# Moving the second token block's divisions among the first block's output products, and reordering copies, additions and loads in the first feed-forward units

## The chip, the core and the metric

The kernel runs on one core of one Trainium2 chip. Its five engines are named as in the profile: PE (TensorE, matrix products; PEld is its weight load), DVE (VectorE), ACT (ScalarE), POOL (GpSimd) and SP (SyncE, which here issues most of the DMAs). The metric is the device time of one execution in microseconds (us). Each engine runs its own list of instructions strictly in order and waits at semaphores for the others; a DMA queue, too, is served by an engine that waits in order before it issues.

## The reference

Two branches read the same `x` (2048 tokens, D = 576) and are mixed by a gate per token:

```python
g = _sigmoid((x * gate_w).sum(-1, keepdims=True))
a = _A_ref(x, A_wqkv, A_w_phi, A_wo)
b = _B_ref(x, B_W_gate, B_W_up, B_W_down)
return g * a + (1 - g) * b
```

`_A_ref` is linear attention with 32 heads of 18. Queries and keys go through a small matrix per head, `w_phi`, and become features `phi = concat(softmax(p), softmax(-p))`. Then `kv = phi_k^T v`, `z = sum phi_k`, `o = (phi_q kv) / (phi_q z + 1e-6)`, and the result is `o @ wo`. `_B_ref` is a gated unit of width F = 4608: `relu(x W_gate) * (x W_up)`, times `W_down`. Everything is float32.

## The kernel before, in words

**Split products.** A float32 operand is cut into a high part (a copy in the reduced format `fp32r`, made by ACT) and a low part (operand minus high part, made by DVE), and one product becomes three matmuls: high by high, high by low, low by high. So before any operand can be multiplied, an ACT copy and a DVE subtraction have to be done.

**Attention.** Tokens are handled in tiles of 128 and blocks of 512 (`TB`). There are four blocks, taken in the order `BLOCKS = (3, 0, 1, 2)`; below "block b" is the b-th of that order, so b = 0 is the first one finished. For each block:
- `sums(b, ...)` (L553 to L574) multiplies the turned query features with the key-value matrix in six groups, ACT copies numerators and denominators out of PSUM, and SP moves the denominators into the tile `dn` by DMA.
- `gather(b, ...)` (L576 to L587) moves leftover numerator rows to their place, by SP's DMAs.
- `invert(b)` (L596 to L601) makes the reciprocals on DVE and sends them to `kt` by a DMA of SP; `split_inverse(b)` (L603 to L616) splits them on POOL into the tile `rd` (for b = 0 the low part is made by DVE).
- `divide(b, k)` for k = 4, 3, 2, 1, 0 is `quotient` (one matmul with `spread`, L634, that lays the reciprocals out over 128 rows, and one DVE product `R`, L636) and `operand_rows` (ACT's high part `oh`, L643, and DVE's low part, L644: `ol` for k < 4, the lower half of `oh` for k = 4). The matmul's PSUM bank is `kv_bank(0)`, except that block 1's last division, k = 0, takes `kv_bank(1)`; later blocks alternate between the two.
- Block 0's output products are accumulated in five banks `PW[0]` to `PW[4]` at once: `first_out(k, mm)` (L652 to L657) multiplies by the weights of row group k for each m of `mm`. `PW[0]` and `PW[1]` are the halves of one PSUM tile `two`; `PW[2]` and `PW[3]` are `kv_bank(1)` and `kv_bank(2)`. `rows_out(b, m, ps)` (L791 to L800) copies a finished bank out on ACT (`o`, L796 and L798; for m = 4 DVE adds two halves, L799) and stores it in the DRAM tile `att`. The other blocks use `project_out(b, m)`, all k in one go, L175.

Meanwhile the last query tiles are finished: `final = query_steps(FIRST - 1)` is a generator with the steps projection; maxima and minima; subtraction and exponentials; and finally sum (`sm`, L204), reciprocals (L357, L358) and scaling (`e`, L209). `hg = half_gates(1)` (L301 to L314) makes square roots of the gate for the second half of the tokens: an ACT square root (L308), which needs its table loaded, and some small DVE operations.

**Feed-forward.** The hidden dimension is cut into 36 chunks, and tokens into two halves of 1024, which gives 72 units. A unit multiplies with seven products instead of eight (a Strassen-like scheme of block sums, order `SEQ = (1, 5, 6, 2, 7, 3, 4)`), so `step(u, j)` has j = 0 to 6. Product 1 goes to a new bank `cx`, 5 to `ca`, 2 to `cy`; 6, 7 and 4 are added to `cx`, 3 to `ca`. Between them the running sums are taken out: `g1` is a copy of `cx` after j = 0 (ACT, L1299, traced at j = 1), `u2` one of `ca` (j = 2), `g2` one of `cx` (j = 3); DVE adds `cy` to `g1` (L1418, j = 4), `cx` to `u2` (L1420, j = 5), `ca` to `g2` (L1423, j = 6), and gates them (L1295). PE may not write the next product into a bank before it is read. In the same step the next unit's weights are made: `blocks` (high part `wb`, L874, and low parts L877 and L880), `sums_of_blocks` (four DVE operations on `wr`, L895 to L898) and `block_sums` (`ws`, same lines). They are kept in DRAM (`wbd`, `wsd`) for the second half. The weight tiles `wb` and `ws` have two buffers each, so unit 2's take those of unit 0. From unit 2 on, the down product of a pair of units is added (`ac`, L1179) to the accumulators, which are first loaded from `att` by `load_acc` (L1141) and `load_rest` (L1146), into the buffers that held the output projection's weights.

The seven token operands of the first half are made during the last projections: `operand_ahead(i)` for i = 0 to 2, `high_in_place(0, i)` (ACT, L856 and L857) and `low_of_place(i)` (DVE, L861 and L841) for i = 3 to 6; `in_place(6)` is both.

**What sets the order.** A planner with estimated durations orders the instructions of each engine, starting from the order of the program text. `in_order(tc, nc, engines...)` pins the listed engines to the order of the text: in the attention part around the change these are PE, SP and POOL, so that DVE and ACT are left to the planner; from `project_out(2, 1)` on, all five are pinned. `after(tc, nc, engine, *firsts)` only says that what is traced inside stands behind the given instructions on that engine, and `last_of(nc, engine)` is the last one traced.

Of the kernel before, what the change touches and what calls it, by code (L numbers as in the profile page):

```python
# [83 lines left out]
def gated_mix_kernel(  # L84
# [603 lines left out]
    with in_order(tc, nc, nc.tensor, nc.sync, nc.gpsimd):  # L688
        F_ = lambda: whole(late[0])
        run(key_steps, t - 1, (T_(t - 3, 2),), T_(t - 3, 1), F_, K_(t - 3), T_(t - 3, 0))  # L690
        run(query_steps, t - 1, (), F_, T_(t - 2, 2))
        run(key_steps, t, (T_(t - 2, 1),), V_(t - 1, 0), F_, K_(t - 2), T_(t - 2, 0), V_(t - 1, 1))
        run(query_steps, t, (V_(t, 0),), V_(t, 1), F_, K_(t - 1), T_(t - 1, 2), K_(t))
        kv_out()
        A2.close()
        PP.append(RS.enter_context(tc.tile_pool(name="ph1", bufs=1, **R_)))
        kb = RS.enter_context(tc.tile_pool(name="kb", bufs=1, **R_))
        rb = RS.enter_context(tc.tile_pool(name="rb", bufs=2, **R_))
        table = kb.tile([QK, P], F32, name="table")[:, :QG + 4]
        nc.sync.dma_start(table, mask_d)  # L700
        mask, hm, eps = table[:, :QG], table[:, QG:QG + 3], table[:, QG + 3:]
        kvm = kb.tile([QK, NQ * QM + 64], F32, name="kvm")[:, :NQ * QM].rearrange("p (g c) -> p g c", g=NQ)
        nc.gpsimd.memset(kvm, 0.0)
        fetch(BLOCKS[1])
        turn2 = lambda u, b: turn(u, b, kv_bank(2)[:QK].rearrange("p (g t) -> p g t", g=4))

        def middle():
            next(late[0])
            next(late[0])
            turn(t - 1, 1)  # L710
            for q in (2, 1, 0):
                kv_turn(q)

        last = query_steps(FIRST - 2, middle, nc.vector)
        next(last)
        for q in (2, 1, 0):
            kv_blocks(q)
        hg = half_gates(1)
        next(hg)
        turn(t - 1, 0)  # L720
        whole(late[0])
        turn2(t, 2)
        turn(t, 1)
        turn2(t, 0)
        next(last)
        next(last)
        two = pp.tile([P, 2, TB], F32, name="po", tag="pp")
        sums(0, (4,), (kv_bank(0),))
        sums(0, (5,), (kv_bank(1),))
        sums(0, (3, 2), (two[:, 0], two[:, 1]))  # L730
        gate_rows()
        sums(0, (1,), (kv_bank(2),))
        sums(0, (0,), (pv1.tile([P, TB], F32, name="po", tag="pv1"),))
        whole(last)
        turned = lambda ps: ps[:QK].rearrange("p (g t) -> p g t", g=4)
        turn_all(FIRST - 2, [(0, turned(kv_bank(0))), (1, turned(kv_bank(1))), (2, turned(kv_bank(2)))])
        final = query_steps(FIRST - 1, eng=nc.vector)
        next(final)
        gather(0, 4)
        invert(0)  # L740
        gather(0, 3, 2, 1, 0)
        inverse = split_inverse(0)
        next(inverse)
        fetch(BLOCKS[2], nc.gpsimd)
        store_turned(FIRST - 2, nc.gpsimd)
        two = pp.tile([P, 2, TB], F32, name="po", tag="pp")
        sums(1, (4,), (kv_bank(0),))
        sums(1, (5,), (kv_bank(1),))
        halves = last_of(nc, nc.scalar), last_of(nc, nc.vector)
        sums(1, (3, 2), (two[:, 0], two[:, 1]))  # L750
        next(final)
        next(final)
        exps = last_of(nc, nc.scalar)
        whole(inverse)
        divide(0, 4)
        sums(1, (1,), (kv_bank(2),))
        sums(1, (0,), (pv1.tile([P, TB], F32, name="po", tag="pv1"),))
        divide(0, 3)
        two = pp.tile([P, 2, TB], F32, name="pw", tag="pp")
        PW = [two[:, 0], two[:, 1], kv_bank(1), kv_bank(2), pv1.tile([P, TB], F32, name="pw", tag="pv1")]  # L760
        first_out(4, range(5))
        divide(0, 2)
        gather(1, 4)
        with after(tc, nc, nc.vector, last_of(nc, nc.vector)):
            invert(1)
        gather(1, 3, 2, 1, 0)
        with after(tc, nc, nc.vector, halves[1]):
            whole(final)
        first_out(3, range(5))
        two = pp.tile([P, 2, TB], F32, name="po", tag="pp")  # L770
        operands(BLOCKS[3])
        turn_all(FIRST - 1, [(2, turned(kv_bank(0))), (0, turned(two[:, 0])), (1, turned(two[:, 1]))])
        divide(0, 1)
        with after(tc, nc, nc.scalar, exps, halves[0]), after(tc, nc, nc.vector, halves[1]):
            whole(hg)
        A.close()
    L_ = dict(reuse_waits="tile")
    xo = ctx.enter_context(tc.tile_pool(name="xo", bufs=3, **L_))
# [173 lines left out]
    with in_order(tc, nc, nc.tensor, nc.sync, nc.gpsimd):  # L952
# [5 lines left out]
        sums(2, (4, 5), halves)  # L958
        divide(0, 0)
        first_out(1, range(3))  # L960
        sums(2, (3, 2), halves)
        first_out(1, range(3, 5))
        sums(2, (1, 0), halves)
        gather(2, 4)
        for m in range(5):
            first_out(0, (m,))
            rows_out(0, m, PW[m])
            if m in (0, 1, 3):
                divide(1, (4, 3, None, 2)[m])
        divide(1, 1)  # L970
        divide(1, 0)
        with after(tc, nc, nc.vector, last_of(nc, nc.vector)):
            invert(2)
        gather(2, 3, 2, 1, 0)
# [24 lines left out]
    with in_order(tc, nc, nc.tensor, nc.vector, nc.scalar, nc.gpsimd, nc.sync):  # L999
# [36 lines left out]
        sums_of_blocks(1)  # L1036
        high_in_place(0, 4)
        project_out(3, 2)
        block_sums(1, high_w)
        low_of_place(4)  # L1040
        high_in_place(0, 5)
        project_out(3, 3)
        low_parts(block_sums, 1)
        low_of_place(5)
        in_place(6)
        project_out(3, 4)
    AP.close()
    BS.close()
# [278 lines left out]
    def step(u, j):  # L1327
# [60 lines left out]
        if make:  # L1388
            if j == 0:
                blocks(v, high_w)  # L1390
                if v + 1 < NC:
                    load_w(v + 1)
            elif j == 1:
                blocks(v, low_w)
                blocks(v, low_w_rows)
            elif j == 2:
                if v < NC - 2:
                    nc.sync.dma_start(wbd[v], WB.pop(v).bitcast(F32))
                sums_of_blocks(v)
            elif j == 4:  # L1400
                block_sums(v, low_w)
                block_sums(v, low_w_rows)
            elif j == 5:
                if v < NC - 2:
                    nc.sync.dma_start(wsd[v], WS.pop(v).bitcast(F32))
        elif j == 0 and NC < u < 2 * NC - 1:
            load_operands(v)
# [10 lines left out]
            tt(out=T["g1"], in0=cy, in1=T["g1"], op=ADD)  # L1418
        elif j == 5:
            tt(out=T["u2"], in0=cx, in1=T["u2"], op=ADD)  # L1420
        elif j == 6:
            a = T["g2"]
            tt(out=a, in0=ca, in1=a, op=ADD)  # L1423
# [24 lines left out]

        swap_in(u, j)
        if u == 0:  # L1450
            if 3 <= j < 5:
                plain_down(0, (high, low)[j - 3])
            elif j == 5:
# [2 lines left out]
        if u == 1 and j < 2:  # L1456
            (nc.sync.dma_start(wbd[u], WB.pop(u).bitcast(F32)) if j == 0 else
             nc.sync.dma_start(wsd[u], WS.pop(u).bitcast(F32)))
        if u == 1 and j == 6:
            for i in range(8):  # L1460
                load_acc(0, i // 2 % 2, i // 4, i % 2)
            load_rest(0)
        if u in (NC + 1, 2 * NC - 1) and j < 4:
            if j % 2 == 0:
                rest_copy(j // 2)
# [172 lines left out]
```

## Time and profile before

| | us |
|---|---|
| median of 3 runs | 1583.54 (1583.13 to 1584.26) |
| the profiled execution | 1582.98 |
| its span, first to last instruction | 1581.2 |
| PE busy in the span | 1567.2 |
| DVE busy | 1189.2 |
| ACT busy | 558.6 |
| granted TensorE clock | 1.00 |

Times inside the execution are counted from the start of the span. In a row of the timeline the first number is the start, the second the duration, `out<-in` the tiles written and read, `xN` how many instructions are merged into the row, and the bracket the idle time of the engine before it and what ended that. The attention part around the change runs from about 250 to 290 us, the projections of blocks 1 to 3 up to 338 us, and the feed-forward units from there to the end; each unit has 49 matmuls of `SEQ`, and from unit 2 on the down products come between them.

### The profile page before, as it was taken

Reading aid. Unit: us, or ns where it says so; the run is one execution under the profiler, and the core shown is the slowest. Engines: PE = TensorE matmul, PEld = TensorE weight load, DVE = VectorE, ACT = ScalarE, POOL = GpSimd, SP = SyncE. Lnnn points to the kernel's source line nnn. Section 1 sums busy time; section 2 is a strip of 40 time slices with the busy share of each in tenths; the row PEclk is TensorE's granted clock in tenths of the full one; section 3 lists DMA queues with packets and bytes.
Section 4 is the critical chain, followed back from the end, with each engine's and each line's share of the span. In section 5 each row is a group of like instructions: output and inputs, shape, how many; then the busy total and the mean of one; then the engine's idle time right before and its main releaser. Section 6 shows DMA issues by size and latency. Waiting matters only on the chain.

```text
span 1581.2 us, 20182 instructions
## 1 busy us (share of the span) xinstructions
PE 1567.2 (99%) x7823; PEld 1311.4 (83%) x7823; DVE 1189.2 (75%) x1865; ACT 558.6 (35%) x918; POOL 175.1 (11%) x243
## 2 busy tenths in 40 slices
PE   9999999999999999999999999999999999999998
PEld 9999995677888888888888888888888888888887
DVE  4997775597787877887777777777767777777777
ACT  4344335563333333333333334232232322232321
POOL 0126521110000000000000002111111111111110
PEclk9999999999999999999999999999999999999999
DMA  5365315597755575556545516543443443543432
GB/s 172 108 214 185 146 50 158 168 350 253 256 201 212 212 278 204 201 212 224 196 172 206 220 44 236 191 183 132 153 183 132 162 160 131 178 159 132 185 136 75
DMA packets 64539, 283.38 MB, mean 179 GB/s; under 512 B 6802, under 2 KB 17298, under 8 KB 55740
## 3 DMA queue, kind: packets, MB, share of 16 engines
q1 hardware_dynamic: 61228, 270.34, 47.1%
q0 software_dynamic: 2352, 10.11, 1.9%
q10 hardware_dynamic: 864, 1.65, 0.3%
q8 instruction: 61, 1.00, 0.3%
q14 instruction: 34, 0.28, 0.1%
HBM read 172.07 MB, written 108.60 MB: 178 GB/s over the span
## 4 chain that ended last, share of the span: by engine, by line
PE 95%; DVE 3%; ACT 1%; DMA 0%; issue 0%; POOL 0%; SPq 0%; ACTq 0%; POOLq 0%
PE cx L1133 28%; PE ca L1133 14%; PE pd L1173 12%; PE pd L1196 10%; PE cy L1133 7%; PE kv L175 4%; PE pk L175 3%; PE pq L175 3%; PE pm L1173 2%; PE pm L1196 2%; PE kv L421 1%; PE po L562 1%; PE pv L237 1%; PE ptr L379 1%; PE pw L175 1%; PE psf L259 1%
## 5 line engine op out<-in xcount | busy, mean ns | idle before, releaser
L1238 ACT ACTIVATE hh<-g 128x512 fp32r<-128x512 f32 x195 | 120.0, 624 | 457.3 <-DVE g L1295 287.9
L1211 DVE TENSOR_TENSOR ac<-pd,ac 128x512 f32<-128x512 f32 x238 | 163.9, 689 | 144.4 <-PE pd L1196 144.2
L1133 PE MATMUL cx<-xo,ws 128*128 128x512 f32 x1008 | 252.0, 389 | 1.6 <-ACT g L1299 1.6
L1133 PE MATMUL ca<-xo,ws 128*128 128x512 f32 x1008 | 251.9, 389 | 0.0
L1133 PE MATMUL cx<-xo,wb 128*128 128x512 f32 x1008 | 249.0, 389 | 1.5 <-DVE u L1420 1.5
L1133 PEld LDWEIGHTS cx<-xo,ws 128*128 128x128 f32 x1008 | 189.2, 188 | 41.2 <-ACT g L1299 2.1
L1133 PEld LDWEIGHTS cx<-xo,wb 128*128 128x128 f32 x1008 | 188.2, 188 | 42.4 <-DVE u L1420 1.9
L1133 PEld LDWEIGHTS ca<-xo,ws 128*128 128x128 f32 x1008 | 189.2, 188 | 39.3
L1173 PE MATMUL pd<-hh,wd 128*128 128x512 f32 x576 | 200.7, 389 | 0.0
L1196 PE MATMUL pd<-hh,wd 128*128 128x512 f32 x476 | 185.2, 389 | 0.0
L1179 DVE TENSOR_TENSOR ac<-pd,ac 128x512 f32<-128x512 f32 x144 | 99.0, 688 | 105.6 <-PE pd L1173 102.8
L1243 DVE TENSOR_TENSOR hl<-g,hh 128x512 fp32r<-128x512 f32 x195 | 135.4, 694 | 1.9 <-ACT hh L1238 0.2
L1299 ACT ACTIVATE g<-cx 128x512 f32<-128x512 f32 x144 | 85.0, 590 | 129.2 <-PE cx L1133 129.1
L1173 PEld LDWEIGHTS pd<-hh,wd 128*128 128x128 f32 x576 | 108.1, 188 | 22.5
L1133 PE MATMUL cy<-xo,wb 128*128 128x512 f32 x504 | 125.9, 389 | 0.0
L1096 ACT ACTIVATE wd<-wdr 128x384 fp32r<-128x384 f32 (+1 forms) x106 | 62.3, 606 | 143.2 <-DMA wdr<-wd 143.2
L1173 PE MATMUL pd<-hl,wd 128*128 128x512 f32 x288 | 112.0, 389 | 0.0
L1133 PEld LDWEIGHTS cy<-xo,wb 128*128 128x128 f32 x504 | 94.6, 188 | 19.6
L1196 PEld LDWEIGHTS pd<-hh,wd 128*128 128x128 f32 x476 | 89.4, 188 | 18.5
L1196 PE MATMUL pd<-hl,wd 128*128 128x512 f32 x238 | 92.6, 389 | 0.0
L841 POOL TENSOR_TENSOR xo<-xr,xo 32x512 fp32r<-32x512 f32 x5 | 8.3, 1670 | 614.7 <-PE ca L1133 608.5
L874 ACT ACTIVATE ws<-wr 128x1536 fp32r<-128x1536 f32 x36 | 53.7, 1491 | 48.2 <-DVE wr L898 46.0
(256 smaller groups left out, 2572.1 us busy)
## 6 DMA issues: line engine op xcount, KB each, us to landing
wsd<-ws SPq DMA_DIRECT2D x34, 1280.0 KB
ws<-wsd SPq DMA_DIRECT2D x34, 1280.0 KB
wbd<-wb SPq DMA_DIRECT2D x34, 960.0 KB
wb<-wbd SPq DMA_DIRECT2D x34, 960.0 KB
wr<-wgu SPq DMA_DIRECT2D x36, 768.0 KB
wdr<-wd SPq DMA_DIRECT2D x36, 576.0 KB
eT<-et SPq DMA_DIRECT2D x10, 594.0 KB
xt<-xb SPq DMA_DIRECT2D x7, 768.0 KB
```

The costliest lines, as they stand in the source:

```text
L175: nc.tensor.matmul(ps, w, m, start=i == 0, stop=i == len(pairs) - 1)
L237: nc.tensor.matmul(pv[i][c], m, w_[:, k, cs], start=k == 0 and n == 0, stop=k == 4 and n == 1)
L874: nc.scalar.activation(o[:, :, 0:3], a, AF.Copy)
L1096: nc.scalar.activation(o[:, 0], a, AF.Copy)
L1133: nc.tensor.matmul(ps, w, v, start=first and m == 0, stop=m == len(pairs) - 1, skip_group_check=True)
L1173: nc.tensor.matmul(ps, w, v, start=k == 0 and (i < 2 or first), stop=k == len(mms) - 1 and (i < 2 or last), skip_group_check=True)
L1179: tt(out=a, in0=ps, in1=a, op=ADD)
L1196: mm = lambda ps, w, v, a, z: nc.tensor.matmul(ps, w, v, start=a, stop=z, skip_group_check=True)
L1211: tt(out=a, in0=ps, in1=a, op=ADD)
L1238: nc.scalar.activation(h, src, AF.Copy)
L1243: tt(out=l, in0=src, in1=h.bitcast(F32), op=SUB)
L1299: nc.scalar.activation(a, ps, AF.Copy)
```

## The change

It has two parts. In the attention part, block 1's divisions k = 4 and k = 3 move ahead, each in front of a `sums(2, ...)`, and the remaining three go behind m = 0, 2 and 4 of block 0's last products; the copy of `PW[0]` is traced behind the product into `PW[1]`. The rest of `final` is held on DVE behind the first division of block 0 (`split`) instead of behind an earlier operation; the rest of `hg` is traced before block 0's division k = 1 and held behind `split` and behind the ACT copy of the division k = 2 (`rows`).

In the feed-forward part, operand 5's ACT copies move in front of operand 4's DVE work and of block sums 1; `in_place(6)` moves from the last projections into unit 0 (j = 1); in unit 1 the low parts of block sums 2, and their store, move from j = 4 and 5 to behind the addition into `u2` at j = 5; and the ten loads of the accumulators move from the end of unit 1 (j = 6) to the start of unit 0 (j = 0).

```diff
@@ -746,13 +746,12 @@
         sums(1, (4,), (kv_bank(0),))
         sums(1, (5,), (kv_bank(1),))
-        halves = last_of(nc, nc.scalar), last_of(nc, nc.vector)
         sums(1, (3, 2), (two[:, 0], two[:, 1]))
         next(final)
         next(final)
-        exps = last_of(nc, nc.scalar)
         whole(inverse)
         divide(0, 4)
+        split = last_of(nc, nc.vector)
         sums(1, (1,), (kv_bank(2),))
...
         first_out(4, range(5))
         divide(0, 2)
+        rows = last_of(nc, nc.scalar)
         gather(1, 4)
...
         gather(1, 3, 2, 1, 0)
-        with after(tc, nc, nc.vector, halves[1]):
+        with after(tc, nc, nc.vector, split):
             whole(final)
         first_out(3, range(5))
...
+        with after(tc, nc, nc.scalar, rows), after(tc, nc, nc.vector, split):
+            whole(hg)
         divide(0, 1)
-        with after(tc, nc, nc.scalar, exps, halves[0]), after(tc, nc, nc.vector, halves[1]):
-            whole(hg)
         A.close()
...
         sums(2, (4, 5), halves)
         divide(0, 0)
         first_out(1, range(3))
+        divide(1, 4)
         sums(2, (3, 2), halves)
         first_out(1, range(3, 5))
+        divide(1, 3)
         sums(2, (1, 0), halves)
         gather(2, 4)
         for m in range(5):
             first_out(0, (m,))
-            rows_out(0, m, PW[m])
-            if m in (0, 1, 3):
-                divide(1, (4, 3, None, 2)[m])
-        divide(1, 1)
-        divide(1, 0)
+            if m > 0:
+                for i in (0, 1) if m == 1 else (m,):
+                    rows_out(0, i, PW[i])
+            if m in (0, 2, 4):
+                divide(1, 2 - m // 2)
...
         high_in_place(0, 4)
         project_out(3, 2)
+        high_in_place(0, 5)
+        low_of_place(4)
+        project_out(3, 3)
         block_sums(1, high_w)
-        low_of_place(4)
-        high_in_place(0, 5)
-        project_out(3, 3)
         low_parts(block_sums, 1)
         low_of_place(5)
-        in_place(6)
         project_out(3, 4)
...
             elif j == 4:
-                block_sums(v, low_w)
-                block_sums(v, low_w_rows)
+                if u > 1:
+                    block_sums(v, low_w)
+                    block_sums(v, low_w_rows)
             elif j == 5:
-                if v < NC - 2:
+                if 2 < v < NC - 2:
                     nc.sync.dma_start(wsd[v], WS.pop(v).bitcast(F32))
...
         elif j == 5:
             tt(out=T["u2"], in0=cx, in1=T["u2"], op=ADD)
+            if u == 1:
+                block_sums(v, low_w)
+                block_sums(v, low_w_rows)
+                nc.sync.dma_start(wsd[v], WS.pop(v).bitcast(F32))
...
         if u == 0:
+            if j == 0:
+                for i in range(8):
+                    load_acc(0, i // 2 % 2, i // 4, i % 2)
+                load_rest(0)
+            elif j == 1:
+                in_place(6)
             if 3 <= j < 5:
                 plain_down(0, (high, low)[j - 3])
...
-        if u == 1 and j == 6:
-            for i in range(8):
-                load_acc(0, i // 2 % 2, i // 4, i % 2)
-            load_rest(0)
```

## The prediction, made before the changed kernel was run

> **What bounds the kernel now.** I read the page first: the engines' busy shares.
>
> ```profile
> PE 1567.2 (99%) x7823; PEld 1311.4 (83%) x7823; DVE 1189.2 (75%) x1865; ACT 558.6 (35%) x918; POOL 175.1 (11%) x243
> ```
>
> TensorE (PE) is the bound, and the change neither adds nor removes a matmul. It can only fill or open holes in PE's row, so next come PE's two longest waits after its start, and the busy time by stretches.
>
> ```profile
> PE cx L1133 <- ACT g L1299: 1.6, 1, 1.6
> PE cx L1133 <- DVE u L1420: 1.5, 1, 1.5
> ```
> ```profile
> 338.00:365.00 27.00, 23.86 (x105) 19.07 (x104) 21.94 (x31) 13.95 (x21) 1.09 (x2) 1.00 0.76 308
> 365.00:1560.00 1195.00, 1195.00 (x5272) 988.45 (x5271) 908.66 (x1423) 386.31 (x637) 81.95 (x158) 1.00 0.50 182
> ```
>
> The second column of the lower fence is PE's busy time: from 365 us on it has no hole, so a hole removed before that stays won. Both waits lie where the diff edits, and so do those of some 0.5 that the timeline shows with their full size. Fourteen matmuls of 512 columns in 3.34 us, the last lasting 0.39, make a pitch of (3.34 - 0.39)/13 = 0.227 us. Whatever lies between two starts beyond 0.227 per matmul is lost.
>
> ```profile
> 277.28 0.40 PE L634 MATMUL kv<-rd,spread 128*128 128x512 f32 x1
> 278.22 0.50 PE L657 MATMUL pw<-oh,wo 128*128 128x512 f32 x1 [0.55 <-ACT o L796]
> ...
> 281.16 0.40 PE L657 MATMUL pw<-ol,wo 128*128 128x512 f32 x1
> 281.88 0.74 PE L634 MATMUL kv<-rd,spread 128*128 128x512 f32 x2 [0.32 <-DVE R L636]
> ...
> 284.09 0.40 PE L175 MATMUL kv<-oh,wo 128*128 128x512 f32 x1
> 285.02 0.50 PE L175 MATMUL kv<-oh,wo 128*128 128x512 f32 x1 [0.53 <-ACT oh L643]
> 285.74 0.50 PE L175 MATMUL kv<-ol,wo 128*128 128x512 f32 x1 [0.23 <-DVE ol L644]
> ...
> 287.09 1.93 PE L562 MATMUL po<-ph,kvm 108*64 108x512 f32 x6
> ...
> 349.76 3.34 PE L1133 MATMUL cx<-xo,wb 128*128 128x512 f32 x14
> ```
>
> Lost here: 0.94 - 0.23 = 0.71 before 278.22, 0.49 before 281.88, 0.70 and 0.49 before 285.02 and 285.74. That is **2.4 us** in the loop of the first block's last output products.
>
> **Part 1: the second block's divisions** (k = 4 and 3 go ahead of two `sums(2, ...)`, the other three to m = 0, 2, 4). One division is one matmul, three operations of 0.6 to 0.7 us on DVE and ACT, and no DMA; SP and POOL are not touched. Two spread matmuls (0.23 each) move 3 to 6 us ahead in PE's order, which costs nothing in total; their operand `rd` comes from POOL:
>
> ```profile
> 269.04 1.29 POOL L612 TENSOR_TENSOR rd<-kt,rd 32x512 fp32r<-32x512 f32 x1
> 271.39 1.08 PE L562 MATMUL po<-ph,kvm 108*64 108x512 f32 x4
> ```
>
> It is done at 270.3, and PE would come to the spread where `sums(2, (3, 2))` now starts, at 271.4; 1 us is left. What each hole turns into:
> - 0.71: PE waited for the copy `o` of bank PW[0], which shares a tile with PW[1]. Now both copies are traced behind both products. The wait goes.
> - 0.49: the spreads of k = 2 and k = 1 use one bank back to back; now two products (1.4 us) lie between, against 0.4 of matmul and 0.68 of DVE. Gone.
> - 1.19: the projection of block 1 reached k = 1 and 0 before their quotients were split. Now only k = 0 comes last: 0.4 matmul, 0.7 `R`, 0.6 `oh`, 0.7 `ol` = 2.4 us, against eleven matmuls of the projection ahead of it, 2.5 us. Just covered.
> What is late next is ACT: five copies `o` and three `oh` at 0.60 (the row of `g` in part 3) are 4.8 us, while PE has 14 products and 3 spreads, 3.9 us, and eleven matmuls more, 2.5, before it needs the last. If they come in a bad order, PE waits for PW[2] or PW[3] by up to 1 us. So this part gives 1.5 to 2.6 (2.4 and the refill after each hole); I take **2.2**, near the upper end, because each cover is there by the rows.
>
> **Part 2: the tail of `final` and `hg`, held behind the first division.**
>
> ```profile
> 255.36 0.50 PE L634 MATMUL kv<-rd,spread 128*128 128x512 f32 x1
> 256.32 1.20 PE L657 MATMUL pw<-oh,wo 128*128 128x512 f32 x4 [0.45 <-DVE oh L644]
> ...
> 258.72 0.39 PE L657 MATMUL pw<-oh,wo 128*128 128x512 f32 x1
> 259.19 0.50 PE L657 MATMUL pw<-ol,wo 128*128 128x512 f32 x1
> ```
> ```profile
> 254.21 1.33 DVE L204 TENSOR_REDUCE sm<-e 128x64 f32<-128x1152 f32 x1
> 255.58 0.69 DVE L644 TENSOR_TENSOR oh<-R,oh 64x512 fp32r<-64x512 f32 x1
> ```
> ```profile
> 256.10 1.28 ACT L308 ACT_TABLE_LOAD   x1
> 257.39 0.21 ACT L308 ACTIVATE gates<-gates 128x8 f32<-128x8 f32 x1
> ...
> 262.80 0.49 ACT L388 ACTIVATE ph<-kv 108x384 f32<-108x384 f32 x1 [2.40 <-PE kv L379]
> ```
>
> Holes of 0.73 and 0.24. The reduction of 1.33 stands between a quotient and its split; `split` forbids that, so the split can come 0.6 sooner. The table load for the square root stands ahead of the copy of k = 3; `rows` puts it behind the copy of k = 2, into 2.4 us in which ACT is idle (the last row). DVE and ACT are not pinned in this block, so the planner may put the reduction in front of the next quotient instead: first split done at 255.65, then 1.3 for the reduction, 0.7 + 0.6 + 0.7 for quotient and split, and 0.7 for the scaling if that comes in front as well, is 259.65, 0.46 later than PE's 259.19. Bounds: -0.46 to +0.75; I take **0.4**, nearer the gain, since one of the two costs moves for certain. The Trainium skill (ScalarE: Activation LUTs, "What ACT_TABLE_LOAD costs") adds a drain of 1.38 us to each switch. Here the square root follows the load's 1.28 at once, so no drain shows; with it, the moved load would overrun that idle time by some 0.5, and the term would be about 0 and the sum below 5.1, still inside the forecast.
>
> Everything between 287 and 338 us hangs on chains that start from PE's own products (sums, gather, inverse, spread), so it moves along whole.
>
> **Part 3: `in_place(6)`, the block sums and the loads of the accumulators.**
>
> ```profile
> 339.89 1.75 PE L1133 MATMUL ca<-xo,ws 128*128 128x512 f32 x7
> 343.28 1.89 PE L1133 MATMUL cx<-xo,ws 128*128 128x512 f32 x7 [1.64 <-ACT g L1299]
> ...
> 359.28 1.75 PE L1133 MATMUL ca<-xo,ws 128*128 128x512 f32 x7
> 362.53 3.49 PE L1133 MATMUL cx<-xo,wb 128*128 128x512 f32 x14 [1.50 <-DVE u L1420]
> ```
> ```profile
> 340.42 1.04 ACT L856 ACTIVATE xo<-xo 128x1024 fp32r<-128x1024 f32 x1
> 341.37 0.61 ACT L857 ACTIVATE xo<-xr 128x512 fp32r<-128x512 f32 x1
> ...
> 342.63 0.60 ACT L1299 ACTIVATE g<-cx 128x512 f32<-128x512 f32 x1
> ```
> ```profile
> 340.88 1.23 DVE L861 TENSOR_TENSOR xo<-xo 128x1024 fp32r<-128x1024 f32 x1
> ...
> 359.24 1.22 DVE L877 TENSOR_TENSOR ws<-wr,ws 128x1024 fp32r<-128x1024 f32 x1 [1.61 <-ACT ws L874]
> 360.48 0.68 DVE L880 TENSOR_TENSOR ws<-wr,ws 32x512 fp32r<-32x512 f32 x1
> ...
> 361.80 0.68 DVE L1420 TENSOR_TENSOR u<-cx,u 128x512 f32<-128x512 f32 x1
> ```
>
> First hole: 343.28 - (339.89 + 7 x 0.227) = 1.80. ACT made two copies of `in_place(6)` (1.6 us) ahead of copying `cx`, and before that operand 5's two behind the block-sum copy. After the change operand 5's copies come earlier, where ACT waits for DVE's sums of blocks, operand 6's stand behind `g`, and `g` can run when its product is done (339.89 and 0.16 for the last matmul's rest). The hole goes. What is late next is DVE: operand 5's and 6's low parts (the shapes of the two `ws` rows, 1.9 each), the add of `o` 0.6, `g` 0.7, the low parts of `wd` 1.4 and `u` 0.7 run back to back from 340.9 to 348.1, and product 4 of unit 0 waits for `u`; by PE's pitch it could start at 347.8. So this gives 349.76 - 348.1 = **1.6**, not 1.8. Second hole: 362.53 - (359.28 + 1.59) = 1.66. The two operations on `ws` (1.9 us) now stand behind `u`, which then ends 0.7 before PE needs it; `ws` is done about 2 us before unit 2's second product reads it, and its store, issued there too, is needed by nobody before unit 4. Gives **1.6**.
>
> The ten loads of the accumulators (8 x 256 KB and 2 x 128 KB, 2.36 MB) move from unit 1's end to unit 0's start on SP's in-order queue. They pass the stores of units 0, 1 and 2 and the load of weights 3, and their buffers come free only when the last projection is done, at 338.5 (339.89 less one product of 1.59, and 0.2 for the last matmul's rest).
>
> ```profile
> 361.64 5.70 SPq L1141 DMA_DIRECT2D ac<-att  x8
> ```
> ```profile
> 369.84 0.69 DVE L1179 TENSOR_TENSOR ac<-pd,ac 128x512 f32<-128x512 f32 x1 [2.65 <-DMA ac<-att]
> ```
> ```profile
> DMA packets 1484, 3.93 MB, mean 280 GB/s; under 512 B 172, under 2 KB 172, under 8 KB 1355
> ```
> ```profile
> 351.95 1.15 ACT L874 ACTIVATE wb<-wr 128x1152 fp32r<-128x1152 f32 x1
> ```
>
> DVE's 2.65 us goes, but cost PE nothing. New: unit 0's `wb` store (0.98 MB), now ahead of the loads, lands behind them, and unit 2's `wb` copy (351.95, then about 350.1) writes the same buffer. At the 280 GB/s of the stretch that holds the loads now (361 to 375), 2.36 + 0.98 MB end at 338.5 + 11.9 = 350.4. ACT has about 0.6 in hand (one copy) before PE waits for the next `g`, so the point is 350.7: there is next to no cover left, and each us beyond costs one. I take **-0.3**. The Trainium skill (DMA: Bandwidth & Descriptors, "Queues, rings and completion order") says that each DMA engine takes a queue's descriptors in ring order, which speaks against this move; its "Where 436 GB/s comes from" gives some 358 GB/s for transfers between HBM and SBUF, and by it the store would end at 347.8 and cost nothing, which makes the sum 5.8.
>
> **The sum.** 2.2 + 0.4 + 1.6 + 1.6 - 0.3 = 5.5 us. The profiled execution took 1582.98 (span 1581.2 and 1.8 around it), so 1577.5; the median shown, 1583.54, is 0.56 above it, which makes **1578.0**.
>
> **Rivals.**
> - *The queue decides.* The accumulators' loads hold back the `wb` store, ACT stands, and PE's copy of `cx` behind it. For it: next to no cover. Against it: rates over 300 GB/s in the stretch 338 to 365 (308 in the row above). At one to four us late, 1579 to 1582.
> - *The same, on the other side.* At 5.8 us past 350.7, that is 356.5, all gains are gone; it needs (2.36 + 0.98 MB)/18 us = 186 GB/s or less, or a wait for the last projection's own store in front of the loads. Against it: the loads' first wait is for PE alone, and the rows they read are those of blocks 1 and 2, stored before that projection began. Time 1584 to 1589.
> - *The divisions do not do what they should.* The planner orders DVE and ACT so that the holes reappear elsewhere: parts 1 and 2 give 0.5 together. 3.4 us won, 1580.1.
>
> **Chances.** Forecast (1576.7 to 1579) 0.60; late queue 0.17; divisions without effect 0.13; slower 0.10. The range goes from all holes gone (6.8 us, 1576.7) with a little beyond, 1576.5, to the late queue at 4 us, 1582.3. About 0.2% (3.2 us, to 1580.4) is what a measurement of this kernel can tell from no change. Faster by more: 0.60 + 0.07 + 0.06 = 0.73; within: 0.10 + 0.07 = 0.17; slower: 0.10.
>
> **What would show it.** Part 1: no wait of `pw` on `o`, and the projection of block 1 without holes. Part 2: `sm` behind the first split, `ACT_TABLE_LOAD` behind the copy of k = 2. Part 3: `g` before operand 6's copies, `u` before `ws`, no PE hole over 0.5 us between 335 and 362; the `wb` copy of unit 2 directly behind `hh`. Wrong would be a wait of that copy on a DMA, a new PE wait at the early spread of k = 4 for `rd`, or one for PW[2] or PW[3] on ACT.

## The result, and the profile after

| | before | after |
|---|---|---|
| median, us | 1583.65 (1582.98 to 1585.32, 13 runs) | 1579.79 (1578.47 to 1581.88, 13 runs) |
| ratio to before | | 0.9976, 95% interval 0.9969 to 0.9983 |
| profiled execution, us | 1582.98 | 1581.88 |
| its span, us | 1581.2 | 1579.4 |
| first spread matmul, us | 253.09 | 255.17 |
| from there to the end, us | 1328.11 | 1324.21 |

The change wins 3.9 us by the medians; 5.5 were predicted. The spans differ by 1.8 only, because this one execution of the changed kernel reached the first spread matmul 2.08 us later. That is not the change: m_order, one of the kernels below, has the same program text up to there and reaches it at 253.20, and all of them together at 253.0 to 255.3. From the first spread matmul (L634, near which the change begins to act) to the end, the profile shows 1328.11 - 1324.21 = 3.90 us, as the medians do. All comparisons below are therefore made on stretches that start there.

The engines' busy shares of the changed kernel. PE runs the same 7823 matmuls as before.

```profile
PE 1568.7 (99%) x7823; PEld 1313.6 (83%) x7823; DVE 1190.2 (75%) x1865; ACT 558.3 (35%) x918; POOL 175.7 (11%) x243
```

Its PE waits, summed (us in total, times, longest). The two of 1.6 and 1.5 that the prediction began with are gone; one of 0.9 is new in the place of the first, but it stands elsewhere, in unit 1. The one of 0.5 on `o` has moved from L657 to L175, in the rows at 284 us below.

```profile
PE cx L1134 <- ACT g L1300: 0.9, 1, 0.9
```

By stretches (length, then PE's busy time), the feed-forward start still has a hole of a microsecond, and what follows has none:

```profile
340.00:367.00 27.00, 26.02 (x114) 20.87 (x112) 22.61 (x32) 12.86 (x19) 0.55 (x1) 1.00 1.00 384
367.00:1560.00 1193.00, 1193.00 (x5263) 986.79 (x5262) 907.70 (x1421) 383.99 (x633) 82.20 (x158) 1.00 0.49 180
```

**Four stretches.** Two groups of six `po` products (L562) stand in both kernels at the same place of PE's order, and cut the attention part in two. PE's timeline of the kernel before, and then of the kernel after:

```profile
253.09 0.47 PE L634 MATMUL kv<-rd,spread 128*128 128x512 f32 x1
...
267.00 1.93 PE L562 MATMUL po<-ph,kvm 108*64 108x512 f32 x6
```
```profile
255.17 0.47 PE L634 MATMUL kv<-rd,spread 128*128 128x512 f32 x1
...
268.39 1.93 PE L562 MATMUL po<-ph,kvm 108*64 108x512 f32 x6
...
287.47 1.93 PE L562 MATMUL po<-ph,kvm 108*64 108x512 f32 x6
```

With 287.09 of before (quoted in the prediction), stretch A, to the first group, is 13.91 before and 13.22 after; stretch B, to the second, 20.09 and 19.08. The table gives these for every kernel that was run, in us, with C from the second group to the first feed-forward product, D from there to the first down product (`pd`), and then from `pd` to the end. `dn` is the start of the reciprocal of block 1's denominators (L599 on DVE), counted from the first spread. It waits there for the DMA that brings them, except in all_three and fetch_behind, where it begins right behind another division of DVE. Each row is one execution.

| kernel | A | B | C | D | `pd` to end | dn | sum |
|---|---|---|---|---|---|---|---|
| before | 13.91 | 20.09 | 51.21 | 29.15 | 1213.75 | 11.66 | 1328.11 |
| after | 13.22 | 19.08 | 51.18 | 26.98 | 1213.75 | 12.22 | 1324.21 |
| attn_only | 13.22 | 19.09 | 51.20 | 29.17 | 1213.73 | 12.19 | 1326.40 |
| ff_only | 13.93 | 20.11 | 51.17 | 26.81 | 1214.21 | 11.89 | 1326.23 |
| divisions_only | 13.94 | 18.43 | 51.24 | 29.16 | 1214.18 | 12.42 | 1326.95 |
| pins_only | 13.21 | 20.88 | 51.20 | 29.16 | 1213.85 | 12.31 | 1328.31 |
| m_order | 13.22 | 17.63 | 51.16 | 27.35 | 1213.75 | 11.81 | 1323.11 |
| late_invert | 13.22 | 19.88 | 51.20 | 26.53 | 1213.75 | 12.76 | 1324.57 |
| stores_first | 13.23 | 22.45 | 52.07 | 25.79 | 1214.52 | 14.11 | 1328.07 |
| all_three | 13.22 | 17.68 | 51.23 | 25.79 | 1214.09 | 12.14 | 1322.01 |
| loads_late | 13.21 | 18.74 | 51.19 | 25.79 | 1215.27 | 11.82 | 1324.21 |
| loads_early_only | 13.91 | 20.38 | 51.23 | 29.16 | 1213.78 | 13.20 | 1328.46 |
| two_fixes | 13.22 | 17.33 | 51.19 | 25.82 | 1213.80 | 11.22 | 1321.36 |
| fetch_behind | 16.15 | 20.28 | 51.92 | 25.79 | 1214.33 | 12.14 | 1328.47 |

So of the 3.90 us, A gave 0.69, B 1.01, D 2.17, and C and the rest nothing. The prediction had 2.6 for A and B together (parts 1 and 2) and 2.9 for D (part 3): it was 0.9 too high in the one and 0.7 in the other.

**What stands late in B.** PE, DVE and ACT of the changed kernel, in that order:

```profile
270.25 0.50 PE L634 MATMUL kv<-rd,spread 128*128 128x512 f32 x1
270.71 0.50 PE L657 MATMUL pw<-oh,wo 128*128 128x512 f32 x1
271.43 0.50 PE L657 MATMUL pw<-ol,wo 128*128 128x512 f32 x1 [0.22 <-DVE ol L644]
...
282.55 0.39 PE L657 MATMUL pw<-ol,wo 128*128 128x512 f32 x1
283.08 0.50 PE L634 MATMUL kv<-rd,spread 128*128 128x512 f32 x1
284.09 0.96 PE L175 MATMUL kv<-oh,wo 128*128 128x512 f32 x3 [0.50 <-ACT o L796]
```
```profile
267.39 0.95 DVE L599 RECIPROCAL dn<-dn 128x128 f32<-128x128 f32 x1 [4.38 <-DMA dn<-R]
268.26 0.11 DVE L310 TENSOR_SCALAR gates<-gates 128x8 f32<-128x8 f32 x1
...
269.22 0.17 DVE L314 TENSOR_SCALAR gates<-gates 128x8 f32<-128x8 f32 x1
269.30 0.69 DVE L636 TENSOR_TENSOR R<-kv,R 128x512 f32<-128x512 f32 x1
270.69 0.69 DVE L644 TENSOR_TENSOR ol<-R,oh 128x512 fp32r<-128x512 f32 x1 [0.70 <-ACT oh L643]
```
```profile
280.94 0.60 ACT L796 ACTIVATE o<-pw 128x512 f32<-128x512 f32 x1 [0.71 <-PE pw L657]
281.43 0.62 ACT L643 ACTIVATE oh<-R 128x512 fp32r<-128x512 f32 x1
281.95 0.59 ACT L796 ACTIVATE o<-pw 128x512 f32<-128x512 f32 x1
282.43 0.60 ACT L796 ACTIVATE o<-kv 128x512 f32<-128x512 f32 x1
282.91 0.64 ACT L643 ACTIVATE oh<-R 128x512 fp32r<-128x512 f32 x1
283.43 0.61 ACT L796 ACTIVATE o<-kv 128x512 f32<-128x512 f32 x1
```

Two places. At 270.7 PE reaches the products of division k = 1 of block 0 before its `ol` is done: 0.23 and 0.49 are lost. Its spread matmul had started at 264.79, but its quotient `R` (269.30) stands on DVE, which works in order, behind the reciprocal, which itself had waited 4.38 us for a DMA, and behind five small operations of `hg` (L310 to L314, 268.26 to 269.39). And at 283 PE loses 0.30 and 0.78: ACT's first copy could not start before the product into PW[1] was done, since PW[0] and PW[1] are one tile, and from then on ACT works without a gap on the five `o` and three `oh`, until 285.18, so that the banks PW[2] (copied until 283.03) and PW[3] (until 284.04) come free too late.

**What stands late in D.** PE, ACT and one row of DVE at the feed-forward start of the changed kernel:

```profile
346.59 1.75 PE L1134 MATMUL ca<-xo,ws 128*128 128x512 f32 x7
348.45 3.47 PE L1134 MATMUL cx<-xo,wb 128*128 128x512 f32 x14
351.76 1.75 PE L1134 MATMUL ca<-xo,ws 128*128 128x512 f32 x7
354.38 1.89 PE L1134 MATMUL cx<-xo,ws 128*128 128x512 f32 x7 [0.87 <-ACT g L1300]
...
359.29 1.75 PE L1134 MATMUL ca<-xo,ws 128*128 128x512 f32 x7
360.88 1.30 PE L1134 MATMUL cx<-xo,wb 128*128 128x512 f32 x5
```
```profile
340.44 0.60 ACT L1300 ACTIVATE g<-cx 128x512 f32<-128x512 f32 x1 [0.89 <-PE cx L1134]
340.94 1.05 ACT L856 ACTIVATE xo<-xo 128x1024 fp32r<-128x1024 f32 x1
...
349.83 0.63 ACT L1239 ACTIVATE hh<-g 128x512 fp32r<-128x512 f32 x1 [4.47 <-DVE g L1296]
352.16 1.17 ACT L874 ACTIVATE wb<-wr 128x1152 fp32r<-128x1152 f32 x1 [1.70 <-DMA wbd<-wb]
353.23 0.61 ACT L1239 ACTIVATE hh<-g 128x512 fp32r<-128x512 f32 x1
353.75 0.58 ACT L1300 ACTIVATE g<-cx 128x512 f32<-128x512 f32 x1
```
```profile
347.72 0.68 DVE L1422 TENSOR_TENSOR u<-cx,u 128x512 f32<-128x512 f32 x1
```

The copy `g` now comes ahead of operand 6's (340.44, 340.94), and the hole behind it is gone. Before product 4 of unit 0 there is 348.45 - 346.59 - 1.59 = 0.27, the wait for `u` (done at 348.40) that the prediction expected. The hole at unit 1's end (1.66) is gone: 360.88 - 359.29 = 1.59. New is 354.38 - 351.76 - 1.59 = **1.03**: ACT waited 1.70 us for the store of `wb` to land, and `hh` and `g` stood behind that copy.

### The profile page after: what moved, and what is told of

The parts are those of the page before. It is cut to its first block, busy times and chain, and to the rows that moved or that the text cites. A ratio compares the mean times of both kernels' runs of the same rounds, so it can differ in the third digit from the quotient of the medians.

```text
span 1579.4 us, 20181 instructions
## 1 busy us (share of the span) xinstructions
PE 1568.7 (99%) x7823; PEld 1313.6 (83%) x7823; DVE 1190.2 (75%) x1865; ACT 558.3 (35%) x918; POOL 175.7 (11%) x243
## 4 chain that ended last, share of the span: by engine, by line
PE 95%; DMA 2%; DVE 2%; ACT 1%; issue 0%; POOL 0%; SPq 0%; DVEq 0%; ACTq 0%; POOLq 0%
PE cx L1134 28%; PE ca L1134 14%; PE pd L1174 12%; PE pd L1197 10%; PE cy L1134 7%; PE kv L175 4%; PE pk L175 3%; PE pq L175 3%; PE pm L1174 2%; PE pm L1197 2%; PE kv L421 1%; PE pv L237 1%; PE po L562 1%; PE ptr L379 1%; PE pw L175 1%; PE psf L259 1%
## 5 line engine op out<-in xcount | busy, mean ns | idle before, releaser
L1100 DVE TENSOR_TENSOR wd<-wdr,wd 128x384 fp32r<-128x384 f32 (+1 forms) x106 | 68.7, 663 | 1.4 <-ACT wd L1097 1.4
```

Of the source, the lines that this page charges most:

```text
L1100: tt(out=o[:, 1], in0=a, in1=o[:, 0].bitcast(F32), op=SUB)
```

## The experiments

Times below are medians with the ratio to the kernel before, run beside it on the same chip. They scatter by 1 us and more from run to run, and no kernel's interval lies clear of that of the kernel after on the faster side (stores_first has the same ratio, 0.9976). So what one edit does is read from the stretches, which are those of one execution each.

**1 and 2. Each part alone.** attn_only is the kernel before with the edits of the attention part, ff_only with those of the feed-forward part (the diff cut at `high_in_place(0, 4)`).

> Only the attention part of the change (divisions of block 1, split, rows). Measured from the start of block 0's first spread matmul to the end of the span, which leaves out the start (the kernel before: 1328.1 us, the changed one: 1324.2). Theory, every part gives what its holes show: 0.7 from the first divisions and 1.0 from the last products, so 1326.4, ratio 0.999. Rival, the attention part's gain is given back before the feed-forward units: 1328.1, ratio 1.000.

> Only the feed-forward part. Theory: 1.8 for unit 0's first hole, 1.5 for unit 1's, less 1.2 for the new hole behind the accumulators' loads, so about 1326.1 from the first spread to the end. Rival, all of the gain comes from here: 1324.2.

attn_only: 1582.58, ratio 0.9989 (0.9980 to 0.9997), and 1326.40. ff_only: 1581.81, ratio 0.9987 (0.9978 to 0.9995), and 1326.23. The profiles add up: 1.71 + 1.88 = 3.6 of 3.90, and of what ff_only lacks, 0.46 lies behind `pd` (1214.21). The two halves don't disturb each other.

**3. The divisions without the pins.** The kernel before with only block 1's divisions moved.

> Only the divisions of block 1 moved; final and hg pinned as before. Measured from the first spread to the first feed-forward product (the kernel before 85.2, with the whole attention part 83.5). Theory, what split and rows win at 2 to 6 us is lost again at 15 us, where PE meets a quotient that stands behind the DMA of the denominators: the divisions alone give nearly all, 83.5 to 83.8. Rival, the two parts add up as 0.7 and 1.0: 84.2.

Its one execution took 1584.31 (the kernel before beside it had a median of 1584.93). A is that of before and B 18.43, 1.66 less. **Part 1 alone is worth 1.66.**

**4. The pins without the divisions.** The kernel before with only this (and `halves` and `exps` dropped):

```diff
         divide(0, 4)
+        split = last_of(nc, nc.vector)
...
         divide(0, 2)
+        rows = last_of(nc, nc.scalar)
...
-        with after(tc, nc, nc.vector, halves[1]):
+        with after(tc, nc, nc.vector, split):
             whole(final)
+        with after(tc, nc, nc.scalar, rows), after(tc, nc, nc.vector, split):
+            whole(hg)
         divide(0, 1)
-        with after(tc, nc, nc.scalar, exps, halves[0]), after(tc, nc, nc.vector, halves[1]):
-            whole(hg)
```

> Only split and rows, the divisions where they were. Theory: the first two holes shrink by 0.8, and a hole of 0.5 to 0.7 appears before the low part of block 0's division k = 1; first spread to first feed-forward product 85.0 to 85.2. Rival, the gain stays: 84.5.

Its one execution took 1584.04. A is 0.70 shorter, as it should be, and B 0.79 longer. Its PE timeline shows where that went, the same place as in the kernel after:

```profile
269.04 0.50 PE L634 MATMUL kv<-rd,spread 128*128 128x512 f32 x1
269.60 0.49 PE L657 MATMUL pw<-oh,wo 128*128 128x512 f32 x1
270.32 0.50 PE L657 MATMUL pw<-ol,wo 128*128 128x512 f32 x1 [0.23 <-DVE ol L644]
```

0.33 and 0.49 are lost there. **Part 2 alone is worth nothing:** it hands back in B what it won in A. Both parts together give 0.69 + 1.01 = 1.70, which is 1.66 and 0.04.

**5. Another order of the last products.** After, with PW[1]'s product moved behind those into PW[2] and PW[3], so that PW[0]'s copy needn't wait for it and the banks come free in the order in which they are wanted:

```diff
-        for m in range(5):
+        for i, m in enumerate((0, 2, 3, 1, 4)):
             first_out(0, (m,))
-            if m > 0:
-                for i in (0, 1) if m == 1 else (m,):
-                    rows_out(0, i, PW[i])
-            if m in (0, 2, 4):
-                divide(1, 2 - m // 2)
+            rows_out(0, m, PW[m])
+            if i in (0, 2, 4):
+                divide(1, 2 - i // 2)
```

> The changed kernel, with block 0's last products in the order m = 0, 2, 3, 1, 4 and each copied at once. Theory, the copy of PW[0] waits for the product into PW[1] of the same tile, and all later copies are late by that: the holes of 0.3 and 0.8 before and in block 1's projection go, 1323.2. Rival, ACT has too many copies there in any order: the hole moves to another bank or to the last quotient, 1324.2.

1578.28, ratio 0.9966 (0.9954 to 0.9978). The holes of 0.30 and 0.78 are gone, as PE's row shows, and B is 17.63, 1.45 less than in the kernel after:

```profile
280.42 0.39 PE L634 MATMUL kv<-rd,spread 128*128 128x512 f32 x1
280.65 0.84 PE L175 MATMUL kv<-oh,wo 128*128 128x512 f32 x3
```

The other 0.4 of the 1.45 is no merit of the edit: the denominators landed 0.41 earlier (dn 11.81), and less was lost at k = 1. So the 1.1 us at 283 was ACT's start and order. The edit changes two things at once, PW[0]'s wait for the product into PW[1] (0.71 us of ACT's time, the bracket at 280.94) and the order in which the banks come free; what each is worth was not separated.

**6. The inverse behind the division.** After, with `invert(1)` and `gather(1, 3, 2, 1, 0)` moved from in front of block 0's division k = 1 to behind it.

> The changed kernel, with block 1's reciprocals traced behind block 0's division k = 1, so that DVE no longer makes that division wait for the DMA of the denominators. Theory: the hole of 0.5 before the low part of k = 1 goes, but PE then comes to the early spread of block 1 before POOL has finished rd and waits there instead, so 1324.1 from the first spread to the end. Rival, rd is in time: 1323.7.

1580.03, ratio 0.9972 (0.9962 to 0.9983). The loss at k = 1 goes, and PE waits for `rd` at block 1's first spread instead:

```profile
272.38 0.49 PE L634 MATMUL kv<-rd,spread 128*128 128x512 f32 x1 [1.20 <-POOL rd L612]
```

B is 19.88, 0.80 longer than in the kernel after. Moved by itself this is no remedy: the reciprocal, which comes when its DMA lands, feeds that spread too. In the kernel after, the loss at k = 1 hides this: POOL's `rd` ends at 273.21 and the spread starts at 273.38; 0.72 sooner, PE would have waited for `rd` by some 0.55 (an estimate from these rows). D is 26.53 here, 0.45 less than in the kernel after; that comes from the landing of the store (see the queue below).

**7. Stores ahead of the loads.** After, with unit 0's stores of `wb` and `ws` issued at j = 0 in front of the accumulators' loads, not at j = 5.

```diff
         if u == 0:
             if j == 0:
+                nc.sync.dma_start(wbd[u], WB.pop(u).bitcast(F32))
+                nc.sync.dma_start(wsd[u], WS.pop(u).bitcast(F32))
                 for i in range(8):
                     load_acc(0, i // 2 % 2, i // 4, i % 2)
...
-            elif j == 5:
-                nc.sync.dma_start(wbd[u], WB.pop(u).bitcast(F32))
-                nc.sync.dma_start(wsd[u], WS.pop(u).bitcast(F32))
```

> The changed kernel, with unit 0's two stores issued in front of the accumulators' loads. Theory, the loads' place in SP's queue is what holds ACT's copy of unit 2's weights: the copy comes at about 350.5, PE's hole of 1.0 in unit 1 goes, 1323.1 from the first spread to the end. Rival, the bytes are too many in any order: the wait moves to another copy or store and the time stays 1324.2.

1579.19, ratio 0.9976 (0.9966 to 0.9985). D is 25.79, 1.19 less than after. ACT's timeline has no wait between `hh` and the copy:

```profile
354.21 0.63 ACT L1239 ACTIVATE hh<-g 128x512 fp32r<-128x512 f32 x1 [4.47 <-DVE g L1296]
354.76 1.17 ACT L874 ACTIVATE wb<-wr 128x1152 fp32r<-128x1152 f32 x1
```

The profiled execution took 1585.14, the longest of its nine, and lost 3.37 in B, more than D won. Its denominators landed late (dn 14.11), PE waited 1.60 at the spread behind the first group, and the granted clock (the column behind POOL's) was below 1 afterwards:

```profile
272.05 0.49 PE L634 MATMUL kv<-rd,spread 128*128 128x512 f32 x1 [1.60 <-DVE R L636]
```
```profile
270.00:272.50 2.50, 0.90 (x3) 0.19 (x1) 1.88 (x8) 0.47 (x1) 0.00 (x0) 1.00 0.09 26
272.50:275.00 2.50, 2.11 (x6) 1.46 (x6) 1.61 (x3) 1.75 (x4) 1.90 (x2) 0.66 0.17 49
```

**8. All three.** After with the edits of 5, 6 and 7.

> Stores in front of the loads, order m = 0, 2, 3, 1, 4, and late reciprocals together. Theory: 1.1 + 1.1 + 0.1 less than the changed kernel's 1324.2, about 1321.9; ratio to the kernel before 0.996. Rival, the waits share one cause behind them (DVE or ACT full): not under 1323.

1577.19, ratio 0.9961 (0.9948 to 0.9973), and 1322.01.

**9. The loads at their old place.** After, with the ten loads back at unit 1, j = 6.

> The changed kernel with the accumulators' loads back at the end of unit 1. Theory: no wait of ACT for the store, DVE waits some 2.6 us for the first accumulator again, at no cost to PE; 1323.1, as with the stores in front. Rival, the early loads were worth something to PE: 1324 or more.

1580.35, ratio 0.9979 (0.9970 to 0.9988). The theory, that the early loads only cost, was wrong. D falls to 25.79, but 1.5 us come back behind `pd`. DVE and PE of this kernel:

```profile
367.01 0.69 DVE L1180 TENSOR_TENSOR ac<-pd,ac 128x512 f32<-128x512 f32 x1 [3.93 <-DMA ac<-att]
```
```profile
371.21 0.50 PE L1174 MATMUL pd<-hh,wd 128*128 128x512 f32 x1 [0.75 <-DVE ac L1180]
...
376.00 1.90 PE L1134 MATMUL cx<-xo,wb 128*128 128x512 f32 x7 [0.18 <-DVE u L1422]
```

PE loses 0.91 and 0.34 there. The first product behind each hole takes some 0.1 longer, and that makes the 1.5. In the kernel before, DVE's wait of 2.65 for the same loads cost PE nothing. Here PE comes to the first `pd` 3.4 us sooner, counted from the first feed-forward product (D), and SP issues the first load only 0.6 sooner (22.7 us behind that product and not 23.3), so the wait of 3.93 reaches PE.

**10. The loads alone.** The kernel before with nothing but the ten loads moved to unit 0.

> The kernel before with nothing changed but the accumulators' loads moved to the start of unit 0. Theory: the wb store lands at about 352.2, and ACT's copy comes to it at 351.95 there, since unit 0 still has its hole of 1.8; so next to nothing is lost, 1328.1 to 1328.4. Rival, the loads cost PE 1 us by themselves: 1329.1.

1584.14, ratio 1.0000 (0.9990 to 1.0009). Without the other edits, unit 2's copy of `wb` comes late enough, 13.65 us behind the first feed-forward product, and the store has landed. So the move of the loads neither wins nor costs by itself. Once the rest of the change has brought both ends forward, it wins 1.5 (`pd` to end, against loads_late) and costs 1.2 (D), next to nothing on balance.

**11. Without the late reciprocals.** After with 5 and 7 only.

> The changed kernel with unit 0's stores in front of the loads and the order m = 0, 2, 3, 1, 4, reciprocals as in the changed kernel. Theory: the late reciprocals gave nothing, since PE only waits for rd instead, so the same as with all three: from the first spread to the end 1322 to 1322.3, ratio 0.996. Rival, they are worth their 0.5: 1322.5 or more.

1577.76, ratio 0.9957 (0.9943 to 0.9971), and 1321.36, the shortest of all. Between 250 and 300 us and between 335 and 375 its PE has none of the waits shown above. Its denominators landed early in that execution (dn 11.22), and k = 1 loses nothing there, so the lead of 0.65 over all_three in the stretches is no merit of the kernel; their intervals don't tell them apart. Both beat the kernel before, and both medians lie below that of the kernel after.

**12. A fetch behind the gathers.** all_three with `fetch(BLOCKS[2], nc.gpsimd)` on SP, behind `sums(1, (0,), ...)`, to have the denominators land sooner.

> All three edits, and the four fetches of block 2's features (2.4 MB) issued by SP behind the small DMAs of block 1's denominators instead of by POOL ahead of them. Theory, the fetch is what holds those small DMAs: DVE's reciprocal starts at about 8 instead of 12 us after the first spread, POOL's rd is done before 16 instead of 18, and PE has no hole at 15 to 19; the sums of block 2 may wait a little for the fetch. 1321.5 to 1322.2 from the first spread to the end. Rival, the small DMAs are slow by themselves: the reciprocal stays at 12.

1583.56, ratio 0.9994 (0.9985 to 1.0004). The theory fell. The six `po` products that need the fetched `ph` came 2.9 us late, and the clock fell behind that hole:

```profile
269.47 3.65 PE L562 MATMUL po<-ph,kvm 108*64 108x512 f32 x6 [2.87 <-issue]
```
```profile
267.50:270.00 2.50, 0.53 (x2) 0.32 (x4) 0.00 (x0) 0.00 (x0) 0.15 (x1) 0.79 0.38 117
270.00:272.50 2.50, 2.50 (x6) 0.46 (x2) 0.00 (x0) 0.00 (x0) 2.42 (x4) 0.50 0.14 33
```

That the hole is the late fetch was only argued: the row names no releaser. Whether the denominators would have come sooner stays open as well, since in this kernel the reciprocal stands directly behind another division on DVE and began without a wait for a DMA.

## Why the prediction was right, and where it was wrong

The direction, the places and most of the steps held: 1579.79 against 1578.0, inside the range of 1576.5 to 1582.3 and 1.8 us above the forecast. The case that had 0.60 (1576.7 to 1579) was missed, though, and two of the three signs that were to show it wrong came: the `wb` copy waited for a DMA, and PE waited for PW[2] and PW[3] on ACT. By steps:

- **Part 1, 2.2: mis-sized, 1.66.** All four holes of before went, and no wait for `rd` came at block 1's early spread in the kernel after. There the cover was 0.17 us (POOL's last `rd` ends at 273.21, the spread starts at 273.38) and not the 1 us of the prediction, and that only because PE had lost 0.72 just before to the same late landing. The failed step is the one that priced ACT: "If they come in a bad order, PE waits for PW[2] or PW[3] by up to 1 us" made the low end of 1.5, and the value was taken near the upper one. The order was bad: 0.30 and 0.78. The sum of ACT's work (4.8 us) was on the safe side, since the eight copies took 4.24. But it let ACT begin with the first product, and the first copy could begin only with the second, for the same reason, the shared tile, that the prediction itself had given for the hole of 0.71. m_order, which takes both the wait and the bad order away, has neither hole.
- **Part 2, 0.4: 0.69 won where it was looked for, and nothing left.** It counted only `final`'s reduction and the table load. `hg` also has small operations on DVE, and these moved too: in the kernel after five of them run from 268.26 to 269.39, between the reciprocal and the quotient of k = 1, so that `R` starts 1.91 us behind the reciprocal's start (269.30 - 267.39). In divisions_only it is 1.19 (267.72 and 268.91). PE comes 0.69 sooner, the quotient 0.72 later, and that is more than was in hand. This is the failed step of the term. The loss then goes with the landing of the denominators: in PE's timelines it is 0.72 with dn at 12.22 (after), 0.82 at 12.31 (pins_only), 0.3 at 11.81 (m_order) and none at 11.22 (two_fixes), about dn less 11.5. The Trainium skill's drain (ScalarE: Activation LUTs, "What ACT_TABLE_LOAD costs"), by which this term would have been about 0, came out at the right number by luck: no drain shows, for in the kernel after the load takes 1.28 from 261.82, and the square root starts at 263.11.
- **Between the parts and the feed-forward: nothing, and nothing it was.** C is 51.21 and 51.18.
- **First and second feed-forward hole, 1.6 and 1.6: right.** 1.80 became 0.27, so 1.53; 1.66 went whole.
- **The queue, -0.3: mis-sized, -1.03 to -1.2 in the kernel after.** The mechanism was right, and so was the point from which it decides: 350.7 is 12.4 us behind the first feed-forward product of the kernel before (338.30); the copy started 13.50 behind it, 1.1 later, and the hole is 1.03. What failed is "2.36 + 0.98 MB end at 338.5 + 11.9". SP's rows of the kernel after:

```profile
336.81 4.69 SPq L1142 DMA_DIRECT2D ac<-att  x8
...
343.74 0.58 SPq L1466 DMA_DIRECT2D wbd<-wb  x1
```

  The first load was issued sooner than the prediction had it, 1.85 us ahead of the first feed-forward product and not 0.2 behind it. But SP came to the store only behind the tenth load, 5.1 us behind that product, where the kernel before has it 5.1 us ahead (333.16), and the copy that waits for the store began at 352.16. These 3.34 MB took 15.35 us, 218 GB/s: the 280 GB/s had been all traffic of its stretch, 3.93 MB, of which the loads were 2.36, and here too other stores and weight loads ran beside them. How much of the delay is SP's queue and how much the transfers' share of the traffic was not separated. All traffic from 340 to 365 us:

```profile
DMA packets 2316, 9.79 MB, mean 392 GB/s; under 512 B 285, under 2 KB 285, under 8 KB 1981
```

  The 358 GB/s that the Trainium skill gives (DMA: Bandwidth & Descriptors, "Where 436 GB/s comes from"), by which the store would have cost nothing, was passed by the traffic as a whole, and didn't help, since the store and the loads were only a part of it. The ring order (its "Queues, rings and completion order") is not shown by itself: with the store in front (stores_first) the wait is gone, but SP's own order, ten issues ahead of the store, would do the same.

  The size is not fixed either. In late_invert, ff_only, the kernel after and m_order, which all have the loads in front, the copy starts 13.06, 13.34, 13.50 and 13.89 us behind the first feed-forward product, against 11.71 in stores_first; D is longer than there by 0.74, 1.02, 1.19 and 1.56. Each time that is 0.6 less than the copy's delay, which is what the prediction had put in ACT's hand.
- **"DVE's 2.65 us goes, but cost PE nothing": right of the kernel before, wrong as a price.** loads_early_only gives 1.0000, but loads_late loses 1.5 from the first additions on. The loads' move was a part of the gain, not only its cost.

Of the rivals, the late queue came true at the small end of its one to four us, and the measured time lies in its 1579 to 1582, though half of the miss is that of parts 1 and 2. Four us late would have been 1581.7 by the rival's own sum (1577.7 without the queue); the upper end of 1582.3 is 0.6 above that. The divisions' rival had 0.5 for these; they gave 1.7. The slow side stayed away: the copy would have had to be 5.8 us late, and was 1.1.

The sum with the measured terms: 1.66 + 0.04 + 1.53 + 1.66 - 1.03 = 3.86, against 3.90.

## What to carry to other kernels

When operations are moved to clear one engine's path, list every engine's share of what moves and look for the next thing in order behind it: here five small DVE operations, at 0.1 to 0.2 us each, gave back the whole gain of their part in an execution whose denominators landed at 12.2. Count the time of a chain of copies from the first one that may start, and not from the first product. A transfer that is moved ahead wants its rate from the traffic that will run beside it there, and the stores that free a double buffer belong in front of it in the queue.

## What was not expected of the hardware

- The small transfers (4 to 12 KB) that bring block 1's denominators land at no fixed time: where DVE's reciprocal waited for them, it began 11.2 to 14.1 us behind the first spread matmul. after and stores_first have the same attention part and show 12.22 and 14.11; before and loads_early_only 11.66 and 13.20. By the losses at k = 1, PE has about 11.5 in hand in the changed kernel and, from loads_early_only alone, about 13 in the kernel before. Why the landing varies was not found.
- Behind PE's holes of 1.6 us in stores_first and 2.9 us in fetch_behind the granted clock fell to 0.66 and 0.50 and came back within 5 to 8 us, so that a hole costs more than its length: stores_first lost 3.37 in B against the kernel after, of which 1.9 is the later landing; the rest lies at 273.4 to 276.9 us, where eight products take 3.43 us, against 1.95 in the kernel after (271.43 to 273.38). Behind the holes of 1.8 and 1.66 of the kernel before, in its stretch from 338 to 365 us, the clock is 1.00 throughout, so the length alone doesn't decide. The Trainium skill (TensorE: Matmul & The Clock Gate, "Part 1: The HAM clock gate") has the gate watch PE's activity in windows that run freely, by which the same hole may or may not trip it; no run here shows the windows.
- C is 0.9 and 0.7 longer in stores_first and fetch_behind, whose attention parts ended late, than in all others. In stores_first PE lost most of it from 313 to 314.4 us, before two products with a low part `ol` (at 314.34 the wait ends with DVE's `ol`); in fetch_behind, most of it before a spread at 314.10 that waits for POOL's `rd`. Why these came late was not followed up.
